# A matrix-vector product of 1024 x 1024 in a one-core backward pass: which operand stands in the array and which streams

## The chip, the cores and the metric

The kernel runs on one core of one Trainium2 chip. The metric is the time of one execution on the device, in microseconds (us); the median of three runs stands for the kernel. The profile comes from one further execution of the same program.

## The reference

The reference is one decode step of an adaLN-conditioned transformer block (one token, width 1024) and its backward pass. Cut to what matters here:

```
mod = silu(c) @ w_mod                      # c: 1x1024, w_mod: 1024 x 6*1024
sa, ca, ga, sb, cb, gb = six rows of 1024 of mod
h = layernorm(x) * (1 + ca) + sa
x = x + ga * attention(h)                  # window of 4096 of a cache of 65536, 32 heads, 4 kv heads
h = layernorm(x) * (1 + cb) + sb
x = x + gb * glu_ffn(h)                    # width 3584
outputs: x and the gradients of x, k_cache, v_cache, wq, wo, w_gate, w_up, w_down, c, w_mod
```

The gradient of c needs, for each of its 1024 rows j, the product of row j of w_mod with the gradient of mod. For the first two sections (sa and ca) that gradient is dh1 and dh1 * ln1, where dh1 is the gradient of the first h and ln1 the first normalised row. So the two products can be folded into one: with w01[j, n] = w_mod[j, n] + w_mod[j, 1024 + n] * ln1[n], the part of the gradient is dcs01[j] = sum over n of w01[j, n] * dh1[n]. This product of a 1024 x 1024 matrix with a row is what the change rewrites.

## The kernel before, in words

Everything is in one program with a hand-written order: each engine runs its instructions in the order of the text, and what crosses engines waits on semaphores. PE multiplies, DVE and ACT move and scale, POOL and SP issue DMAs (POOL on the software queue q0, SP on the hardware queue q1). The outputs are large, above all the two cache gradients (64 MB each), most of which is zeros; the zeros are written all through the run between other transfers. The last pieces of zero are issued on POOL at 459.36 us of the span; after that every transfer is a result that some engine has to make first.

The stretch around the change is the last 90 us of the span. What stands there, in the order of the text:

- `sec(j)` (eight of them): DVE reduces a product with a row (`ttr`, L255), makes an outer product of 128 x 4096 (`outer_dve`, L251), POOL stores it, 1 MB (L1253). `dwq_tile(j)`: an outer product of 128 x 4096 on DVE and a store of 1 MB (L1301). `s2(j)`: an outer product of 128 x 2048 and a store of 0.5 MB (L1305).
- `grad_kv` for the v cache: 32 products of 512 columns on PE (L1288), evacuated by ACT (L1292); then three stores of 1 MB (`kv_store`, L1297).
- `layernorm_bwd_col` (its sums over the partitions by PE, L333, a float32 product), `bcast` (16 products of 128 columns, L346; ACT evacuates, L351).
- **`dcs01 = matvec_T(...)`**, the line of the change. `matvec_T` (L275) has 64 products: block (jb, nb) of the folded matrix `w01_T`, 128 x 128 bf16, is loaded into the array as the weights, and two columns (`dh1_hl[:, nb, :]`, the upper and the lower bf16 half of dh1) stream through. The eight products of one jb add up in PSUM. DVE copies one half (L247) and adds the other (L238).
- `kv_store(out_3, dv_home, 3)` on POOL, then on DVE `sec(7)`, `dwq_tile(3)`, the row x2, two outputs turned by PE (L293), the small sums of the gradient of c (which take `dcs01`), and its output, turned by PE as well.
- `grad_kv` for the k cache: 32 products of 512 columns on PE, evacuated by ACT and DVE in turn; between them DVE makes `dwq_tile(4)` to `dwq_tile(7)` and `s2(0)` to `s2(7)`. `s2(3)` and `s2(4)` write where `sec(7)`'s tile lies, so they wait until its store has landed. The stores go to POOL up to `dwq_tile(5)`, and to SP from `s2(2)` on.
- the last four stores of the k cache, two on POOL and two on SP.

PSUM: the products of 512 columns take their banks from a list of seven that goes round (`new_ps`); small sums take a separate bank (`new_acc`). `scr`, a row of 1024 bf16 per partition, holds `dattn_b` in the last part of the kernel; its last reader there is an outer product of `dwo` on DVE, at 483.5 us.

Of the kernel before, what the change touches and what calls it, by code (L numbers as in the profile page):

```python
# [10 lines left out]
P = 128  # L11
FP32 = mybir.dt.float32
# [8 lines left out]
KD = D // P  # L21
# [40 lines left out]
def kernel(  # L62
# [26 lines left out]
    nc = tc.nc  # L89
# [13 lines left out]
    def ar(off, size):  # L103
        return arena[:, int(off * KIB):int((off + size) * KIB)]
# [4 lines left out]
    def vt(shape, name, dt=FP32):  # L109
        n = shape[1] if dt == FP32 else (shape[1] + 1) // 2  # L110
        if dt not in (FP32, BF16) or n > 48:
            return pool.tile(shape, dt, name=name)
        a = slab[1]
        slab[1] += n
        assert slab[1] <= slab[0].shape[1], slab
        v = slab[0][:, a:a + n]
        return v if dt == FP32 else v.bitcast(BF16)[:, 0:shape[1]]
# [17 lines left out]
    ones_f = vt([P, 1], "ones_f")  # L135
# [83 lines left out]
    def next_pool():  # L219
        nrot[0] += 1  # L220
        return rot[nrot[0] % len(rot)]

    def new_ps(name="ps"):
        p, tag = next_pool()
        return p.tile([P, 512], FP32, name=name, tag=tag)

    def new_bank(name="acc"):
        return pacc.tile([P, 512], FP32, name=name, tag="acc")

    def new_acc(name="acc"):  # L230
        return new_bank(name)[:, 0:64]
# [5 lines left out]
    def tt(out, a, b, op):  # L237
        return nc.vector.tensor_tensor(out=out, in0=a, in1=b, op=op)  # L238
# [4 lines left out]
    def addv(out, a, b):  # L243
        return tt(out, a, b, ALU.add)

    def cp(out, a):
        return nc.vector.tensor_copy(out=out, in_=a)  # L247
# [13 lines left out]
    def hilo(col, n, name):  # L261
        hl = vt([P, n * 2], name, BF16)
        v = hl.rearrange("p (n k) -> p n k", k=2)
        cp(v[:, :, 0], col)
        lo = vt([P, n], name + "_lo")
        tt(lo, col, v[:, :, 0], ALU.subtract)
        cp(v[:, :, 1], lo)
        return v

    def matvec_T(blk, cols, name):  # L270
        ncol = cols.shape[2]
        ps = new_acc("mv_" + name)
        for jb in range(KD):
            for nb in range(KD):
                nc.tensor.matmul(ps[:, jb * ncol:(jb + 1) * ncol], lhsT=blk(jb, nb),  # L275
                                 rhs=cols[:, nb, :], start=(nb == 0), stop=(nb == KD - 1))
        half = ncol // 2
        v = ps[:, 0:KD * ncol].rearrange("p (j n) -> p j n", j=KD)
        res = vt([P, KD * half], name)
        r = res.rearrange("p (j n) -> p j n", j=KD)  # L280
        cp(r, v[:, :, half:ncol])
        addv(r, r, v[:, :, 0:half])
        return r

    def outer_act(out, col, b):
        return nc.scalar.activation(out=out, in_=b, func=ACT.Copy, scale=col)
# [55 lines left out]
    def bcast(col_bf, ncols, out_bf, engs):  # L342
        for k, j0 in enumerate(range(0, ncols, 4)):
            ps = new_ps("bc_ps")
            for jj in range(4):
                nc.tensor.matmul(ps[:, jj * P:(jj + 1) * P],  # L346
                                 lhsT=col_bf[:, j0 + jj:j0 + jj + 1].broadcast_to([P, P]), rhs=ident_bf[:, :],
                                 start=(jj == 0), stop=(jj == 3), skip_group_check=True)
            o = out_bf[:, j0 * P:(j0 + 4) * P]
            if engs[k % len(engs)] == "A":  # L350
                last = nc.scalar.copy(out=o, in_=ps[:, :])  # L351
            else:
                last = cp(o, ps[:, :])
        return last
# [11 lines left out]
    w01_T = ar(128, 16).rearrange("p (n j) -> p n j", n=KD)  # L366
# [193 lines left out]
    for ch in range(8):  # L560
        ps = new_ps("sc_ps")
        for g in range(G):
            mm = nc.tensor.matmul(ps[32 * g:32 * g + 32, 0:512], lhsT=q_col2[:, HG * g:HG * g + 32],
                                  rhs=k_T[:, g, ch * 512:(ch + 1) * 512], start=True, stop=True,
# [157 lines left out]
    for g in range(G):  # L722
        nbank = bank_pair("n_ps", g)
        for t_ in range(KT):
# [7 lines left out]
            for k in range(2):  # L732
                mm = nc.tensor.matmul(nbank[k][:, :], lhsT=k_nat[:, g, t_ * DH:(t_ + 1) * DH],  # L733
                                      rhs=vp[:, t_ % 2, 4 * k:4 * k + 4, :].rearrange("p h d -> p (h d)"),
                                      start=(t_ == 0), stop=False)
# [11 lines left out]
            elif s in (40, 44):  # L747
                j = 6 + (s - 40) // 4
# [3 lines left out]
        for k in range(2):  # L752
            nc.tensor.matmul(nbank[k][:, :], lhsT=nkb_rows[:, :], rhs=bd[:, 4 * k:4 * k + 4, :].rearrange("p h d -> p (h d)"),
                             start=False, stop=True)
# [465 lines left out]
    dattn_b = scr  # L1220
# [75 lines left out]
    def kv_store(og, home, g, queue=nc.gpsimd):  # L1296
        queue.dma_start(out=kv_out(og, g), in_=home[:, g, :])  # L1297
# [11 lines left out]
    for b in range(2):  # L1309
        do4 = new_ps("do4")  # L1310
        for i in range(KD):
            for a in range(4):
                w = wo_t[4 * b + a].rearrange("p a (i d) -> p i a d", i=KD)
                nc.tensor.matmul(do4[32 * a:32 * a + 32, :], lhsT=dattn_bf[:, i:i + 1].broadcast_to([P, 32]),
                                 rhs=w[:, i, :, :], start=(i == 0), stop=(i == KD - 1), tile_position=(0, 32 * a))
        nc.scalar.copy(out=do_sb.rearrange("q (h r a) -> q a h r", h=4, a=4),
                       in_=do4.rearrange("q (a h r) -> q a h r", a=4, h=4))
        for hh in range(4):
            nc.tensor.matmul(dov[:, b, :, hh], lhsT=do_sb[:, hh * P:(hh + 1) * P], rhs=ident_bf[:, 0::32],
                             start=True, stop=True)  # L1320
# [31 lines left out]
    for p in range(NBP):  # L1352
        for it in range(KD):
            nc.tensor.matmul(dh1_ps[:, p:p + 1], lhsT=B_t[p][:, it * P:(it + 1) * P], rhs=dattn_bf[:, it:it + 1],
                             start=(it == 0), stop=(it == KD - 1))
# [16 lines left out]
    zero(Z_ROWS[5])  # L1372
    dw_rows(1, 3, 16, outer_dve)
    dcs234 = matvec_T(lambda jb, nb: w2_t[jb][:, nb * P:(nb + 1) * P], dh2_hl, "dcs234")
    make_bd(DO_bd, do_bf)
    make_bd(Q_bd, q_col2[:, 0:HQ])
    mulv(pd, do_bf, o_col)
    c_ps = new_acc("c_ps")
    for tc_ in range(4):
        nc.tensor.matmul(c_ps[32 * tc_:32 * tc_ + 32, 0:1], lhsT=pd, rhs=ones_f[:, 0:1],  # L1380
                         start=True, stop=True, tile_position=(0, 32 * tc_))
# [18 lines left out]
    dh1_hl = hilo(dh1, KD, "dh1_hl")  # L1400
    for c2 in range(2):
        ps = new_ps("dp_ps")
        for g in range(G):
            for tc_ in range(4):
                t0 = (8 * tc_ + 4 * c2) * P
                nc.tensor.matmul(ps[32 * tc_:32 * tc_ + 32, :], lhsT=do_pad[:, HQ * g:HQ * g + HQ],
                                 rhs=v_nat[:, g, t0:t0 + 512], start=(g == 0), stop=(g == G - 1),
# [21 lines left out]
    dx0 = vt([P, KD], "dx0")  # L1429
    addv(dx0, dx0b, dx1)  # L1430
    bcast(dmod_bf[:, 0:16], 16, dmod_b2, "A")
    dcs01 = matvec_T(lambda jb, nb: w01_T[:, nb, jb * P:(jb + 1) * P], dh1_hl, "dcs01")
    kv_store(out_3, dv_home, 3)
    sec(7)
    dwq_tile(3)
# [5 lines left out]
    dcsum = vt([P, KD], "dcsum")  # L1441
# [6 lines left out]
    ts(t1, t1, 1.0, ALU.add)  # L1448
    mulv(t1, t1, sig_c)
    dct = vt([P, KD], "dct")  # L1450
    addv(dct, dcs01[:, :, 0], dcsum)
    addv(dct, dct, dcs)
    dcv = vt([P, KD], "dcv")
    mulv(dcv, t1, dct)
# [53 lines left out]
```

## Time and profile before

| | us |
|---|---|
| three runs, median (lowest to highest) | 593.28 (592.71 to 594.45) |
| the profiled execution's own time | 593.15 |
| its span (first to last instruction or transfer) | 591.4 |
| the 64 products of L275 on PE, first to last | 535.10 to 536.99 |
| last store issued (POOL) | 571.07 |

The profile gives, for each engine, its busy time, and for each group of instructions what ended the idle time before it. Shares of busy time over the whole span say little here, since stages differ: PE is busy 72% of the span, DVE 60%, ACT 42%, and the DMA engines are at nine tenths or more in all but the first and the last of 40 slices. The views that matter for the change are the timeline from 530 us on, the table of windows of the same stretch (busy time of each engine, granted clock, share and rate of the DMA engines), the source view of single lines (durations, time from the issue of a DMA to its landing) and the DMA view of short windows, which tells which queue's packets moved.

### The profile page before, as it was taken

The numbers are of one execution on the slowest core, as the hardware profiler recorded it, in microseconds if no ns is written. First come the engines' busy times: TensorE is split into PE (matmuls) and PEld (weight loads), VectorE is DVE, ScalarE is ACT, GpSimd is POOL, SyncE is SP. The second block draws the span as 40 slices with busy tenths as digits, with TensorE's granted clock in tenths as the row PEclk, the third lists the DMA queues.
The fourth block names the chain that finished last, engine by engine and source line by source line (L and its number), as shares of the span: only waits on it lengthen the run. The fifth ranks groups of instructions, "written<-read, shape, count | busy, mean of one in ns | idle before, by whom it ended". The sixth has DMA issues, their size and how long they took to land.

```text
span 591.4 us, 10184 instructions
## 1 busy us (share of the span) xinstructions
PE 426.5 (72%) x4167; PEld 245.7 (42%) x4196; DVE 353.6 (60%) x644; ACT 247.9 (42%) x398; POOL 147.3 (25%) x250
## 2 busy tenths in 40 slices
PE   3997779999999999997976856767664447075410
PEld 2784433332334545543544645555552435013100
DVE  3665679988830102039371866877986968555750
ACT  2579511554540103411223655666581456084310
POOL 3112214122122212222222321333212533222100
PEclk9998689999999999998997667786876558555555
DMA  8999999999999999999999999999999999999997
GB/s 348 421 418 423 418 457 423 426 432 434 422 401 462 408 444 427 405 433 442 421 377 414 417 412 410 399 409 402 422 418 423 426 426 423 424 419 415 414 416 313
DMA packets 31903, 246.05 MB, mean 416 GB/s; under 512 B 4765, under 2 KB 4765, under 8 KB 16544
## 3 DMA queue, kind: packets, MB, share of 16 engines
q0 software_dynamic: 26864, 225.98, 94.8%
q1 hardware_dynamic: 4944, 19.41, 9.3%
q8 instruction: 33, 0.54, 0.4%
q14 instruction: 14, 0.11, 0.0%
q10 hardware_dynamic: 48, 0.01, 0.0%
HBM read 88.52 MB, written 185.60 MB: 464 GB/s over the span
## 4 chain that ended last, share of the span: by engine, by line
DMA 36%; PE 27%; DVE 18%; ACT 9%; issue 5%; POOL 1%; ACTq 0%; POOLq 0%; DVEq 0%
DMA out_dram<-out_dram 13%; DMA out_dram<-arena 10%; PE n_ps L733 9%; DMA arena<-in_w_mod_dram 6%; DMA arena<-in_B_w_gate_dram 6%; DVE arena L255 5%; PE b_ps L792 4%; DVE arena L251 4%; PE t_ps L687 4%; DVE scr L255 3%; ACT arena L1292 3%; ACT arena L526 2%; DVE arena L238 2%; ACT arena L695 1%; PE tp_k L505 1%
## 5 line engine op out<-in xcount | busy, mean ns | idle before, releaser
L792 PE MATMUL b_ps<-arena 128*128 128x512 bf16 x493 | 115.3, 382 | 2.6 <-ACT arena L936 1.1
L238 DVE TENSOR_TENSOR arena<-arena 128x2048 bf16<-128x2048 bf16 (+1 forms) x67 | 78.2, 1177 | 9.0 <-PE n_ps L733 5.2
L936 ACT COPY arena<-tp_side 128x1024 bf16<-128x1024 bf16 x62 | 60.8, 1017 | 49.7 <-PE tp_side L935 49.0
L792 PEld LDWEIGHTS <-arena 128*128 128x128 bf16 x512 | 48.7, 99 | 57.6 <-issue 4.6
L733 PE MATMUL n_ps<-arena 128*128 128x512 bf16 x247 | 66.5, 389 | 3.4 <-DVE arena L238 2.5
L202 POOL DMA_DIRECT2D out_dram<-out_dram x72 | 35.7, 496 | 129.5 <-PE n_ps L733 49.6
L251 DVE TENSOR_SCALAR arena<-arena,slab 128x3584 bf16<-128x3584 bf16 (+2 forms) x40 | 43.4, 1120 | 24.1 <-DMA out_dram<-arena 24.1
L935 PE MATMUL tp_side<-ident_bf,arena 128*128 128x128 bf16 x496 | 49.7, 265 | 8.9 <-DVE arena L238 4.5
L935 PEld LDWEIGHTS <-arena 128*128 128x128 bf16 x496 | 41.3, 122 | 17.7 <-issue 9.2
L1288 PE MATMUL ps_kv<-arena 32*128 32x512 bf16 x64 | 26.6, 581 | 28.5 <-DVE arena L259 11.7
L695 ACT CAST arena<-t_ps 128x512 bf16<-128x512 f32 x56 | 28.9, 598 | 39.9 <-PE t_ps L687 39.9
L1292 ACT ACTIVATE arena<-ps_kv 128x512 bf16<-128x512 f32 x48 | 25.0, 723 | 38.8 <-PE ps_kv L1288 19.7
L255 DVE CUSTOM_DVE_ANT_0 arena<-arena,scr 128x1024 bf16<-128x1024 bf16 x35 | 40.8, 1219 | 0.2
L733 PEld LDWEIGHTS <-arena 128*128 128x128 bf16 x256 | 21.5, 99 | 35.4 <-issue 18.9
L255 DVE CUSTOM_DVE_ANT_0 scr<-arena,b1k 128x1024 bf16<-128x1024 bf16 x28 | 34.2, 1222 | 3.1 <-DMA arena<-in_B_w_down_dram 2.6
L247 DVE CAST arena<-b_ps 128x512 bf16<-128x512 f32 x6 | 4.1, 692 | 48.9 <-PE b_ps L792 48.9
L209 POOL DMA_DIRECT2D out_dram<-out_dram x32 | 19.5, 610 | 33.6 <-DVE rows_all L238 25.2
L687 PE MATMUL t_ps<-arena 128*32 128x512 bf16 x256 | 24.1, 399 | 3.3 <-ACT arena L756 2.8
L1288 PEld LDWEIGHTS <-arena 32*128 32x128 bf16 x64 | 6.8, 112 | 47.1 <-issue 46.4
L526 ACT COPY arena<-tp_wq 128x1024 bf16<-128x1024 bf16 x23 | 21.4, 1070 | 7.3 <-PE tp_wq L524 7.3
L1073 ACT COPY arena<-tp_ug 128x1024 bf16<-128x1024 bf16 x21 | 20.5, 1007 | 7.5 <-PE tp_ug L1072 7.5
L1049 PE MATMUL fg<-arena,slab 128*32 128x256 bf16 x224 | 15.1, 404 | 8.2 <-DMA arena<-in_B_w_gate_dram 8.2
(266 smaller groups left out, 649.3 us busy)
## 6 DMA issues: line engine op xcount, KB each, us to landing
out_dram<-arena POOLq DMA_DIRECT2D x35, 1024.0 KB, 14.6
out_dram<-out_dram POOLq DMA_DIRECT2D x32, 1024.0 KB, 12.8
out_dram<-arena POOLq DMA_DIRECT2D x16, 896.0 KB, 17.5
out_dram<-zeros POOLq DMA_DIRECT2D x10, 1024.0 KB, 10.3
arena<-in_A_wq_dram POOLq DMA_DIRECT2D x8, 1024.0 KB, 20.9
arena<-in_A_wo_dram POOLq DMA_DIRECT2D x8, 1024.0 KB, 13.7
arena<-in_w_mod_dram POOLq DMA_DIRECT2D x7, 1024.0 KB, 18.9
arena<-in_B_w_up_dram POOLq DMA_DIRECT2D x14, 512.0 KB, 10.1
```

Source lines behind the costliest of these rows:

```text
L202: ins = nc.gpsimd.dma_start(out=as_rows(region, BIGP).bitcast(FP32), in_=zero_src[:, 0:P * ZW // 4].rearrange("i (p x) -> (i p) x", p=BIGP ...
L238: return nc.vector.tensor_tensor(out=out, in0=a, in1=b, op=op)
L251: return nc.vector.tensor_scalar(out=out, in0=a, scalar1=s1, scalar2=None, op0=op0)
L255: return nc.vector.tensor_tensor_reduce(out=out, in0=w, in1=b, scale=1.0, scalar=0.0, op0=ALU.mult, op1=ALU.add, accum_out=acc)
L687: nc.tensor.matmul(ps[32 * hh:32 * hh + 32, :].rearrange("p (j m) -> p j m", j=4), lhsT=N_sb[:, h * P + a:(h + 1) * P - 3 + a:4], rhs=a4[: ...
L695: nc.scalar.copy(out=o, in_=v)
L733: mm = nc.tensor.matmul(nbank[k][:, :], lhsT=k_nat[:, g, t_ * DH:(t_ + 1) * DH], rhs=vp[:, t_ % 2, 4 * k:4 * k + 4, :].rearrange("p h d -> ...
L792: mm = nc.tensor.matmul(bbank[p][k][:, :], lhsT=a4[:, p, h, :], rhs=wo_t[u][:, a, k * 512:(k + 1) * 512], start=(i == 0 and a == 0), stop= ...
L935: nc.tensor.transpose(tp[:, i * P:(i + 1) * P], blk[:, i * P:(i + 1) * P], ident_bf[:, :])
L936: nc.scalar.copy(out=blk if dst is None else dst, in_=tp[:, :])
L1288: nc.tensor.matmul(ps[:, :], lhsT=rows[r, t8 * P:(t8 + 1) * P], rhs=bd[r, :], start=True, stop=True, tile_position=(32 * tc_, 0))
L1292: nc.scalar.activation(out=o, in_=v, func=ACT.Copy, scale=float(scale))
```

## The change

`dcs01` is made by a new function, in which the two columns of dh1 stand in the array as weights and the folded matrix streams through, 512 columns at a time. Per half h of the 1024 rows j: eight products of 512 columns add up in the first two partitions of a bank; DVE copies the two rows of 512 to SBUF, as float32, into `scr`; four float32 products with a column of two ones turn 128 columns each into a column of 128 partitions and add the two rows. One copy then takes the eight columns out. The addition of the two halves on DVE goes away, since the ones add them. Nothing else is moved; the line numbers behind the new function are 16 higher.

```
+    def matvec_rows(mat, cols, name, room):
+        row = room.bitcast(FP32)[0:2, 0:512]
+        col = new_acc("mc_" + name)
+        for h in range(2):
+            ps = new_ps("mr_" + name)
+            for nb in range(KD):
+                nc.tensor.matmul(ps[0:2, :], lhsT=cols[:, nb, :], rhs=mat(nb)[:, h * 512:(h + 1) * 512],
+                                 start=(nb == 0), stop=(nb == KD - 1))
+            cp(row, ps[0:2, :])
+            for j in range(4):
+                nc.tensor.matmul(col[:, 4 * h + j:4 * h + j + 1], lhsT=row[:, j * P:(j + 1) * P],
+                                 rhs=ones_f[0:2, 0:1], start=True, stop=True)
+        res = vt([P, KD], name)
+        cp(res, col[:, 0:KD])
+        return res
...
-    dcs01 = matvec_T(lambda jb, nb: w01_T[:, nb, jb * P:(jb + 1) * P], dh1_hl, "dcs01")
+    dcs01 = matvec_rows(lambda nb: w01_T[:, nb, :], dh1_hl, "dcs01", dattn_b)
...
-    addv(dct, dcs01[:, :, 0], dcsum)
+    addv(dct, dcs01, dcsum)
```

## The prediction

> **What bounds the kernel now.** I read the busy shares by slice first, then the timeline from 530 us, the table of windows for the same stretch, and the times from issue to landing of the stores. The slices:
>
> ```profile
> PE   3997779999999999997976856767664447075410
> PEclk9998689999999999998997667786876558555555
> DMA  8999999999999999999999999999999999999997
> ```
>
> A digit is tenths of a slice of 14.8 us. The DMA engines are full in all slices but the ends: 246 MB at 416 GB/s fill the span. A delay on another engine costs something only if the transfers run out of work, and it is the last slices that have no zeros left to fill in (the last piece is issued at 459.36). The change lies in slice 37:
>
> ```profile
> 534.99 1.91 PEld L275 LDWEIGHTS <-arena 128*128 128x128 bf16 x64
> 535.10 1.89 PE L275 MATMUL mv_dcs<-arena 128*128 128x2 bf16 x64
> ...
> 537.03 0.17 DVE L247 COPY arena<-mv_dcs 128x8 f32<-128x8 f32 x1 [2.46 <-PE mv_dcs L275]
> ...
> 537.31 1.22 DVE L255 CUSTOM_DVE_ANT_0 g_last<-g_last,arena 128x1024 bf16<-128x1024 bf16 x1
> ...
> 540.03 1.02 POOL L1253 DMA_DIRECT2D out_dram<-arena  x1 [1.77 <-DVE arena L251]
> ...
> 548.60 0.53 POOL L1301 DMA_DIRECT2D out_dram<-arena  x1 [6.84 <-DVE arena L251]
> ...
> 557.63 0.75 DVE L251 TENSOR_SCALAR arena<-arena,slab 128x2048 bf16<-128x2048 bf16 x1 [4.35 <-DMA out_dram<-arena]
> ```
>
> Start and duration in us; in brackets, the idle time before and what ended it. DVE waits for the 64 products and has `sec(7)` behind them (537.31), whose store POOL issues at 540.03. `dwq_tile(3)` follows at 541.23, and then POOL has nothing until `dwq_tile(4)`, 548.60. The 557.63 row is `s2(3)`, which waits for `sec(7)`'s landing. The windows (PE, PEld, DVE, ACT, POOL busy, then granted clock, DMA share, GB/s):
>
> ```profile
> 520.00:530.00 10.00, 9.28 (x19) 1.88 (x19) 5.90 (x6) 9.92 (x21) 2.34 (x3) 0.50 1.02 421
> 535.00:540.00 5.00, 1.99 (x67) 1.90 (x65) 2.94 (x6) 2.81 (x6) 2.10 (x4) 0.50 1.02 415
> 555.00:560.00 5.00, 0.37 (x1) 0.10 (x1) 2.37 (x4) 0.00 (x0) 0.00 (x0) 0.50 1.00 413
> 588.00:591.40 3.40, 0.00 (x0) 0.00 (x0) 0.00 (x0) 0.00 (x0) 0.00 (x0) 0.50 0.11 48
> ```
>
> The clock is 0.50 throughout, and at 535 to 540 the transfers go on at full rate with every engine idle two fifths of the time or more: they live on what was issued earlier.
>
> **What goes.** 64 products in 1.89 us (0.0265 us each at this clock) and one small addition on DVE.
>
> **What comes, on PE and DVE in turn.** A product of 512 columns starts every 0.427 us at this clock (the k-cache products of L1288, from 544.90 on), and the last ends 0.629 us after its start (their duration). Eight take 7 x 0.427 + 0.629 = 3.62. They start at 535.10 as before: their bank was last held by the third from last of the 32 v-cache products, which ACT has evacuated by 534.9. DVE's copy of 512 float32 columns takes 0.69 (the 128x512 f32 copies of L247; 8x128 takes 0.28, so columns set it, not partitions). DVE starts 0.04 behind PE; PE starts 0.12 (L293) to 0.28 (L643) behind DVE, I take 0.2. `scr` was last read at 483.5, so the copy waits for nothing else. Four float32 products are eight passes, as L829 shows two each: 0.11 per pass there at full clock, 0.07 and 0.17 between L333's at half clock, 0.22 if L829's doubles. I take 0.17, L333's own, and keep 0.07 and 0.22. So:
>
> - half one: 535.10 + 3.62 = 538.72; copy to 539.45; turn from 539.65, 8 x 0.17 to 541.0.
> - half two: to 544.62; copy to 545.35; turn from 545.55, seven passes and 0.42 for the last (L333) to 547.2; the copy of eight columns, and `sec(7)` starts at 547.3.
>
> Before it starts at 537.31, so DVE is **10.0 us late** (8.5 with the short passes, 11.0 with the long ones and 0.28). Behind DVE's wait stand `sec(7)`, `dwq_tile(3)`, x2, the sums, the k cache's evacuation and all later outer products; PE's turns and k-cache products stand behind theirs. All of it shifts by 10.0, `dwq_tile(4)`'s issue to 558.6.
>
> **What hides it.** First, `s2(3)`'s wait: its input would be ready at 553.28 + 10.0 = 563.3, `sec(7)` has landed at about 557.6 (below), so from there the chain is only 563.3 - 557.63 = 5.7 late: last stores at 575.7 to 576.8 instead of 570.07 to 571.07. Second, the backlog. Stores on POOL's queue go in order; `sec(7)`, issued at 550.0, still meets the v cache's stores, the last of which lands at 537.73 + 17.34 = 555.06 (L1297's longest). It lands at 557.6 as before, and `dwq_tile(3)` 2.55 later (the spacing of the landings before it), at 560.15; before it takes longer,
>
> ```profile
> L1301 POOL DMA_DIRECT2D out_dram<-arena x1: 532/532/532, 541.2 to 541.2; - x1
> ...
> DMA to landing us min/median/max: 19.7/19.7/19.7
> ```
>
> 541.23 + 19.7 = 560.9, since SP's first store shares the engines from 557.9 on, which it won't now. Then **nothing is queued** until `dwq_tile(4)`.
>
> A store counts as landed when the slowest of its 16 engines is done, and the spread is large: by the trace's landing counts the 16 parts of `dwq_tile(3)` landed between 554.8 and 560.9, half of them by 557.9, and those of the very last store between 584.4 and 590.45. The end is set by the slowest engines (the 588 to 591.4 window: share 0.11). So the faster engines can idle from 555 or 558 to about 560 and still end no later than the slow ones do; only a gap on the slow ones lengthens the run.
>
> Their gap is 558.6 + L - 560.15, L being the time from issue to a first packet on an idle queue. Before shows L from two sides: SP's first load, with idle engines, is issued at 0.74 and has no packet by 1.70 (first at 1.74), so 1.0; the last k-cache stores on POOL are issued at 570.55 and move nothing before 575, while SP's packets fill the engines, so 4.45. The engines that matter are nearly empty, so it is near the first; I take 2.0, for the software queue's issue is longer (0.53 on POOL, 0.33 on SP). Gap: 558.6 + 2.0 - 560.15 = **0.4 us**. Ends: 557.1 + 1.0, no gap; 559.6 + 4.45, 3.9 us.
>
> Later gaps: from 560.6 the stores of `dwq_tile(4)` to `s2(3)` are 4 MB, 10.1 us; the next, `dwq_tile(6)`, is issued at 562.0 + 5.7 = 567.7. No gap there, nor before the last four.
>
> The Trainium skill ("DMA: Bandwidth & Descriptors", Specifications) gives a first-byte latency of about 1 us for a software queue. By it the gap is nil and the time 593.15; the 4.45 us row speaks against it, though for busy engines.
>
> **Sum.** 593.15 (profiled execution) + 0.4 = 593.55; it is 0.13 below the median of the runs, so 593.7.
>
> **Rivals.**
> 1. *The queue runs dry on the slow engines too.* A gap longer than 1.8 us (0.3%, about what a measurement of this kernel can tell from no change) needs delay and L to sum to 13.4 instead of 12.0, as with 10.0 and the 4.45 of the POOL row: 558.6 + 4.45 - 560.15 = 2.9, 596.2; with both at their ends 597.2. For it: that is the only POOL row with an empty queue, and if slow engines are merely behind in turn, the mean one counts (558.6 + 2.0 - 558 = 2.6, 595.9). Against: other queues filled the engines in that row.
> 2. *A shorter delay.* If PE gets its full clock, product starts halve to 0.21: the two halves take about 3.4 us less, the delay is 6.6, `dwq_tile(4)` is issued at 555.2, before the queue empties: 593.3. Against: the clock stays at 0.50 though PE is 9.28 of 10 us busy at 520 to 530. The Trainium skill ("TensorE: Matmul & The Clock Gate", Part 1: The HAM clock gate) says about 3.4 us of sustained matmuls release the clock; by that the 520 window should show it, and it doesn't.
> 3. *Faster.* From 585 on only SP's queue has work, and the rate falls (365 GB/s, then 221, 115, 49): 1.12 MB in 5.4 us that 415 GB/s would move in 2.7. When the faster engines idle at 555 to 560 and the last stores join a shorter SP queue, the end can be more even. Half of the 2.7 gained: 592.0. Against: each engine's bytes are the same.
> 4. *That the change isn't what it says*: excluded by the built order on PE, 16 products of 2x512 and eight of 128x1 in place of 64.
>
> **Chances.** Forecast (gap under 1.8 us) 0.48, rival 2 0.06, both within 0.3%; rival 1 0.38; rival 3 0.08. So faster 0.08, same 0.54, slower 0.38. The range leaves out a tenth at each end: from rival 3's 592.2 to rival 1's 596.8.
>
> **What would show it.** Right: the copy out of the turn at about 547.1 and `sec(7)` at 547.3; PE waiting on DVE twice; `s2(3)` at 563 with no wait on a DMA; a DMA share well below 1 in 555 to 561 alone; last stores issued near 576, the span's end within a microsecond. Wrong: product starts nearer than 0.427 or a granted clock over 0.50 (delay), DMA idle past 561 or in other windows (L, supply), or an end that moves by more than the gap on the engines that end last.

## The result, and the profile after

The median of 22 runs of the changed kernel is **594.06 us** (592.99 to 595.37), that of 22 runs of the kernel before, taken in turn with them, 593.35 us (592.19 to 594.60). The ratio is 1.0015, with a 95% interval of 1.0008 to 1.0021: a little slower, by less than the 0.3% of the forecast's bound. The profiled execution took 594.23 us (before 593.15), and its span is 592.42 us (before 591.37), so 1.05 us more; the medians differ by 0.71 us.

The slices of the page of the changed kernel, in the same rows as before:

```profile
PE   3997689998999999997977756776665447086520
PEclk9997689999999999999998757778777657557555
DMA  8999999999999999999999999999999999999996
```

The fourth digit from the end is the slice of the change. PEclk is 7 there, and was 5. The DMA row differs in the last digit alone.

The timeline of the changed kernel from the first new product on (start, duration, what; in brackets the idle time before and what ended it):

```profile
535.16 3.27 PE L291 MATMUL mr_dcs<-arena 128*2 128x512 bf16 x8
...
538.47 0.68 DVE L247 COPY scr<-mr_dcs 2x512 f32<-2x512 f32 x1 [3.98 <-PE mr_dcs L291]
...
539.21 1.05 PE L295 MATMUL mc_dcs<-slab,scr 2*128 2x1 f32 x8 [0.77 <-DVE scr L247]
...
540.19 1.89 PE L291 MATMUL mr_dcs<-arena 128*2 128x512 bf16 x8
542.11 0.68 DVE L247 COPY scr<-mr_dcs 2x512 f32<-2x512 f32 x1 [2.96 <-PE mr_dcs L291]
...
544.01 1.22 DVE L255 CUSTOM_DVE_ANT_0 g_last<-g_last,arena 128x1024 bf16<-128x1024 bf16 x1
...
546.73 1.02 POOL L1269 DMA_DIRECT2D out_dram<-arena  x1 [8.55 <-DVE arena L251]
...
555.29 0.53 POOL L1317 DMA_DIRECT2D out_dram<-arena  x1 [6.83 <-DVE arena L251]
...
558.03 2.60 DVE L251 TENSOR_SCALAR arena<-arena,slab 128x4096 bf16<-128x4096 bf16 x3
...
572.80 1.05 POOL L1313 DMA_DIRECT2D out_dram<-arena  x2 [12.66 <-issue]
```

The first eight products take 3.27 us and the second eight 1.89, since the granted clock rose at 538.0, near the end of the first eight. `sec(7)` starts at 544.01 instead of 537.31, which makes DVE 6.70 us late, and `dwq_tile(4)` is issued at 555.29 instead of 548.60. At 558.03 the outer products run on with no wait for a DMA: the 4.35 us that `s2(3)` waited before have gone. So the last two stores on POOL start only 2.25 us later than before (572.80 for 570.55).

The windows of the changed kernel (busy PE, PEld, DVE, ACT, POOL, then granted clock, DMA share, GB/s):

```profile
535.00:540.00 5.00, 4.23 (x18) 1.63 (x16) 0.68 (x1) 2.73 (x6) 2.10 (x4) 0.70 1.01 410
540.00:545.00 5.00, 3.12 (x19) 1.72 (x18) 1.75 (x3) 0.00 (x0) 0.00 (x0) 0.98 1.00 418
...
535.10:538.00 2.90, 2.90 (x9) 0.84 (x8) 0.00 (x0) 2.63 (x6) 1.92 (x4) 0.50 0.99 415
538.00:542.00 4.00, 3.23 (x18) 1.55 (x16) 0.68 (x1) 0.00 (x0) 0.18 (x1) 1.00 1.01 408
...
554.00:556.00 2.00, 0.86 (x5) 0.14 (x1) 2.00 (x3) 1.74 (x4) 0.58 (x2) 0.50 0.86 358
556.00:558.00 2.00, 1.02 (x3) 0.48 (x4) 2.00 (x4) 0.41 (x1) 1.02 (x2) 0.50 0.93 381
...
588.00:592.40 4.40, 0.00 (x0) 0.00 (x0) 0.00 (x0) 0.00 (x0) 0.00 (x0) 0.50 0.05 20
```

The kernel before has, at 554 to 558:

```profile
554.00:556.00 2.00, 0.00 (x0) 0.00 (x0) 0.00 (x0) 0.00 (x0) 0.00 (x0) 0.50 1.03 422
556.00:558.00 2.00, 0.00 (x0) 0.00 (x0) 0.37 (x1) 0.00 (x0) 0.00 (x0) 0.50 0.97 406
```

The granted clock is 0.70 and 0.98 at 535 to 545, where it was 0.50. The DMA engines fall to 0.86 and 0.93 at 554 to 558 (before 1.03 and 0.97), a mean idle time of 2 x 0.14 + 2 x 0.07 = 0.42 us. It falls on the fast engines only: `dwq_tile(3)` has landed, on its slowest engine, at 559.64 and `dwq_tile(4)` at 562.16, which is 2.52 us later, the usual spacing of full queues. And in this execution the transfers end **earlier** than in that of the kernel before: SP's last store has landed at 590.06 (before 590.45), with 16 parts that end between 586.79 and 590.06 instead of 584.38 and 590.45.

So the time isn't lost in the transfers. It is lost behind them. The last landing of POOL's queue is the issue of its last store and the time to its landing, 573.33 + 15.07 = 588.40 after and 571.07 + 14.23 = 585.30 before. It moved by 3.10 us, 0.84 more than the issue. The wait for a first packet is not what added this: the first packet of these two stores moved 4.90 us after the first one's issue before (575.45) and 4.96 after (577.76), with SP's packets on the engines until then. The rest passed between that packet and the landing, 9.86 us before and 10.64 after, while SP's queue moved about as many bytes as POOL's; why it took longer is not shown. What follows on POOL is the program's last line. The source view of it in the kernel before, on POOL (shortest, median and longest of three in ns, then when the first and the last start):

```profile
L1503 POOLq DRAIN  x3: 51/93/17575, 571.0 to 591.1; - x3
```

The same view of the changed kernel:

```profile
L1519 POOLq DRAIN  x3: 51/93/18418, 573.2 to 592.1; - x3
```

The longest is the first: POOL waits for its own DMA queue. Before, that ends at 571.0 + 17.6 = 588.5, after at 573.2 + 18.4 = 591.6, both **3.24 us after POOL's last store has landed**. 0.78 us of a last round between the engines follow. On SP, the DRAINs of the kernel before and of the changed one:

```profile
L1503 SPq DRAIN  x3: 7/7/7, 590.5 to 590.8; - x3
...
L1519 SPq DRAIN  x3: 7/7/7, 590.1 to 591.9; - x3
```

Before, SP's last landing (590.45) came later than 588.5 and 0.92 us after it the span was over; now SP is through at 590.2 and waits, and it is POOL's closing that comes last: 588.40 + 3.24 + 0.78 = 592.42, the span. It grew by 1.05 us though every byte was out 0.4 us sooner.

### The profile page after: what moved, and what is told of

Same layout as the page of the kernel before. It is cut to its first block, busy times and chain, and to the rows that moved or that the text cites. A ratio compares the mean times of both kernels' runs of the same rounds, so it can differ in the third digit from the quotient of the medians.

```text
span 592.4 us, 10121 instructions
## 1 busy us (share of the span) xinstructions
PE 432.1 (73%) x4135; PEld 246.2 (42%) x4164; DVE 354.6 (60%) x645; ACT 247.9 (42%) x398; POOL 147.0 (25%) x250
## 4 chain that ended last, share of the span: by engine, by line
PE 44%; DVE 20%; DMA 19%; ACT 7%; issue 6%; POOL 1%; ACTq 0%; POOLq 0%; DVEq 0%
PE b_ps L808 15%; DMA out_dram<-arena 9%; PE n_ps L749 8%; DMA arena<-in_B_w_gate_dram 5%; DVE arena L251 5%; DVE arena L238 4%; PE t_ps L703 3%; DMA arena<-in_w_mod_dram 3%; DVE arena L255 3%; PE ps_kv L1304 3%; DVE scr L255 2%; ACT arena L542 2%; PE bc_ps L362 1%; ACT arena L711 1%; PE tp_k L521 1%
## 5 line engine op out<-in xcount | busy, mean ns | idle before, releaser
L977 POOL DMA_DIRECT2D arena<-in_B_w_up_dram x14 | 10.8, 770 | 42.9 <-DVE slab L255 22.1
## 6 DMA issues: line engine op xcount, KB each, us to landing
arena<-in_w_mod_dram POOLq DMA_DIRECT2D x7, 1024.0 KB, 18.7
```

## The experiments

**Theory A**: POOL's closing step sets the end as soon as POOL's last landing is less than 3.1 us ahead of SP's (4.02 us from landing to end against 0.92); before it was 5.14 ahead, after 1.66. The change only makes POOL's last stores late enough for it. **Theory B**, the rival: the loss is not one of the end. It is what the new products and the transfers around them cost in themselves, with a gap in the supply of the DMA engines where the delay is long enough, and no choice of a queue for the last stores alters it. For the clock, **R**: it rose because the new products fill all 128 rows of the array, where the cache products fill 32; **S**: the rows do not matter, and any products issued as closely as these would raise it.

### The last four stores on another queue, in the changed kernel

```
-        kv_store(out_2, dk_home, g, nc.gpsimd if g < 2 else tail)
+        kv_store(out_2, dk_home, g, tail)
```

> The changed kernel, with the last four stores of the k cache all on SP's queue instead of two on POOL and two on SP. Theory A (closing): in the changed kernel the transfers end as early as before (590.06 against 590.45 us), and the span is longer because POOL's closing step takes 3.24 us after the last store of its own queue has landed, and that landing has moved from 585.30 to 588.40. Then without a late store on POOL the span should end about 0.9 us after SP's last landing, near 591.0, 1.4 us less than the changed kernel: 592.8, ratio to the kernel before 0.998 to 1.000. Theory B (gap, the forecast's own step): the slow DMA engines were short of work at 555 to 560; moving the last stores gives nothing back: 594.1, ratio 1.0015.

Measured 593.36 us (592.82 to 593.74), ratio 1.0002 (0.9993 to 1.0011): level with before, though this interval alone still meets that of the change at its edge. The source view of the last line in this kernel, on POOL:

```profile
L1519 POOLq DRAIN  x3: 51/93/12812, 559.1 to 591.5; - x3
```

The same on SP:

```profile
L1519 SPq DRAIN  x3: 7/7/7, 590.9 to 591.2; - x3
```

POOL's step is over at 559.1 + 12.8 = 571.9 and out of the way. SP's first DRAIN is at 590.9, though its last store landed at 590.03: SP goes through the semaphores of the DMAs in nine steps, one after the other, and its last store's is now in the third, so the six steps behind it come after the landing; before, it was in the last. From the landing to the DRAIN it is 0.87 us instead of 0.09, and 0.45 of it lies between the third step and the fourth, which is not explained here. That is 0.8 us which the change of queue costs in itself, as this run of the kernel before with the same edit shows:

> The kernel before with the last four stores of the k cache all on SP, the control to the same edit of the changed kernel. Theory A (closing): POOL's closing step ends 2 us ahead of SP's last landing there, so that there is nothing to win: 593.2, ratio 1.000. If one queue at the end is better in itself, the ratio is below 0.999, and what the same edit won in the changed kernel was not the closing step.

Measured 594.07 us (592.99 to 594.79), ratio 1.0017 (1.0007 to 1.0027). I had expected no difference: the edit costs the kernel before 0.17%. Its span is 592.68, 1.70 after its last landing at 590.98, where before has 0.92; the rest of the 1.31 us by which the span is longer is a last landing 0.53 us later. So what the edit gives back in the changed kernel is more than the 0.13% seen. To be rid of the 0.8 us, I tried the hardware queue of ACT for the two stores of POOL, in the changed kernel and in the one before:

```
-        kv_store(out_2, dk_home, g, nc.gpsimd if g < 2 else tail)
+        kv_store(out_2, dk_home, g, nc.scalar if g < 2 else tail)
```

> The changed kernel with the two last k-cache stores that POOL issues put on ACT's hardware queue, SP's two left as they are. Theory A (closing): POOL's closing step is done by about 572, and SP's last store is still the last one SP looks at, so the 0.8 us that four stores on SP cost at the end don't come; the span should end about 0.9 us after the last landing near 590.1, at 591.0: 592.7, ratio 0.999. If ACT's queue has a closing step of its own like POOL's, it stays near 1.0015. If late transfers on any queue cost it, likewise.

> The kernel before with the two last k-cache stores that POOL issues put on ACT's hardware queue: the control. Theory A (closing): POOL's closing step was not what ended it (2 us ahead), so nothing to win: 593.0, ratio 1.000, and the changed kernel with the same edit is no slower than this one. If the edit is better in itself, the ratio is under 0.999 here too.

Measured 593.29 us, ratio 0.9999 (0.9990 to 1.0007), and 593.11 us, ratio 1.0003 (0.9993 to 1.0013). The source view of the last line on POOL, in the first and in the second:

```profile
L1519 POOLq DRAIN  x3: 51/93/12122, 559.6 to 591.4; - x3
...
L1503 POOLq DRAIN  x3: 51/102/24205, 552.6 to 591.6; - x3
```

POOL's step is over at 571.7 and 576.8. SP still needed 0.9 us from its last landing to its DRAIN in both (its last store's semaphore was in the third step again), so the 592.7 was not reached. But the pair settles the main point: with POOL's closing out of the way in both, the changed kernel is level with the other one, and its interval doesn't meet that of the change itself (1.0008 to 1.0021). B is out for a delay of this size.

### The closing step alone, in the kernel before

```
-        kv_store(out_2, dk_home, g, nc.gpsimd if g < 2 else tail)
+        kv_store(out_2, dk_home, g, nc.gpsimd)
```

> The kernel before, with the last four stores of the k cache all on POOL's queue. Nothing on PE, DVE or ACT is changed, and no byte more is moved. Theory A (closing): POOL's last landing becomes the last of all, near 590, its closing step ends 3.24 us later, the span near 594: 2.5 us more, 595.9, ratio 1.004. Theory B (gap): the last stores' queue doesn't matter, 593.4, ratio 1.000.

Measured 596.65 us (596.42 to 597.28), ratio 1.0057 (1.0043 to 1.0070). The source view of the last line, on POOL:

```profile
L1503 POOLq DRAIN  x3: 51/102/22138, 571.7 to 594.3; - x3
```

The last byte is out at 590.50, as before (590.45), and POOL's step ends at 571.7 + 22.1 = 593.8, 3.32 us later. No work is changed here, only the queue that lands last, and it costs 0.57%, against 0.4% expected.

### The delay alone, in the kernel before

Fourteen additional outer products of 1024 columns on DVE, where the new products would be, into a row that nothing reads any more; 30 of them in a second kernel.

```
     dcs01 = matvec_T(...)
+    for _ in range(14):
+        outer_dve(scr, ones_f[:, 0:1], dq_b[:, 0:1024])
```

> The kernel before with its 64 products, and 14 additional outer products of 128x1024 on DVE (0.478 us each by the rows of L251) behind the two copies of dcs01: a delay of 6.7 us alone, of the same size as in the changed kernel. They write an unused row. Theory A (closing): the delay alone brings the whole difference: dwq_tile(4)'s store is issued at 555.3, the last stores at 572.3, POOL's last landing is near 588.4 and the time as that of the changed kernel, 594.1, ratio 1.0015. Theory B (gap): 555.3 + 2.0 lies ahead of 560.15, where the slow engines run out, so no gap: 593.4, ratio 1.000. If it is something about the products themselves (their form, or the clock they bring) and not the delay, the ratio is 1.000 too, with POOL's last landing at 585.

Measured 594.74 us (594.23 to 595.13), ratio 1.0024 (1.0016 to 1.0033). The timeline of this kernel:

```profile
537.21 7.26 DVE L251 TENSOR_SCALAR scr<-arena,slab 128x1024 bf16<-128x1024 bf16 x14
544.39 1.22 DVE L255 CUSTOM_DVE_ANT_0 g_last<-g_last,arena 128x1024 bf16<-128x1024 bf16 x1
```

The source view of the last line, on POOL:

```profile
L1505 POOLq DRAIN  x3: 51/93/18742, 573.6 to 592.8; - x3
```

A delay of 7.08 us with the 64 old products gives the loss of the change and 0.09% more, with intervals that meet: POOL's step ends at 573.6 + 18.7 = 592.3, again 3.24 after POOL's last landing (589.10). That is 0.7 us later than in the changed kernel, 0.4 by the later issue and 0.3 by a longer time to landing. The clock stayed at 0.50 in this stretch. So no new product is needed for the loss; lateness of this size is enough.

> The kernel before with 30 additional outer products on DVE behind the copies of dcs01: a delay of 15.2 us (14 of them made 7.1, 0.506 each), past the point from which the slow DMA engines too should run out of work. They write an unused row. With 1.1 us from issue to first packet on an idle queue (seen in the run with 32 rows): sec(7)'s store is issued at 555.2, its first packet comes at 556.3, while the slowest engine is free at about 554.8; dwq_tile(4)'s at 563.8, first packet 564.9, while dwq_tile(3) ends at about 561.4. Theory A (closing) alone: about 3 us, as POOL's last store ends with SP's: 596.4, ratio 1.005. Theory B (gap) alone: 1.5 + 3.5 = 5.0 us, 598.3, ratio 1.0085. Both, one after the other: 8 us, 601.4, ratio 1.0135.

Measured 602.80 us (602.71 to 603.33), ratio 1.0169 (1.0155 to 1.0182), 1.4 us above what I had expected from both theories together. With a delay of 15.9 us (0.4 of it because this execution entered the stretch later) the queues do run dry, twice; windows of this kernel:

```profile
552.00:554.00 2.00, 0.00 (x0) 0.00 (x0) 1.93 (x4) 0.00 (x0) 0.00 (x0) 0.50 0.35 147
554.00:556.00 2.00, 0.00 (x0) 0.00 (x0) 2.00 (x4) 0.00 (x0) 0.06 (x1) 0.50 0.00 0
556.00:558.00 2.00, 0.59 (x2) 0.12 (x2) 1.41 (x5) 0.00 (x0) 1.49 (x2) 0.50 0.31 131
...
562.00:564.00 2.00, 2.00 (x9) 0.83 (x8) 1.84 (x3) 1.49 (x3) 0.00 (x0) 0.50 0.34 133
564.00:566.00 2.00, 0.07 (x1) 0.00 (x0) 2.00 (x4) 1.21 (x3) 1.24 (x3) 0.50 0.30 111
```

What the shares lack of 1 in these five windows of 2 us is 7.4 us, and the last byte is out at 597.53, 7.1 later than before: here the idle time comes out at the end nearly in full. With the closing step in place of SP's end (3.24 + 0.78 - 0.92 = 3.1) that makes the 10.2 us by which the span is longer (601.55). My expectation had both dry spells, at 1.5 and 3.5 us. The second came so: `dwq_tile(4)` landed 5.96 us after `dwq_tile(3)` (569.13 for 563.17) instead of 2.5. The first was too short: no packet moved from 553.8 to 557.5, since the slowest engine was free at 554.1 and not at 554.8, and `sec(7)`'s store, issued at 555.94, had its first packet 1.6 us later and not 1.1.

### The clock: the same products over 32 rows

```
-  nc.tensor.matmul(ps[0:2, :], lhsT=cols[:, nb, :], rhs=mat(nb)[:, h * 512:(h + 1) * 512], ...)
+  nc.tensor.matmul(ps[0:2, :], lhsT=cols[0:32, nb, :], rhs=mat(nb)[0:32, h * 512:(h + 1) * 512], ...,
+                   tile_position=(0, 0))
```

Three quarters of each sum are left out here.

> The changed kernel, its 16 products of 512 columns taking 32 of the 128 rows only, so that three quarters of the sum are left out; the columns that stream, and so the time of a product at a given clock, are the same. Theory R (rows): the clock rose to full at 538 because products on all 128 rows filled the array long enough; the 32-row products of the v cache had not brought it at 520 to 533. Then the clock stays at 0.50, a product starts every 0.427 us, sec(7) starts at 547.3 and dwq_tile(4)'s store is issued at 558.6, as the forecast had it; by theory A (closing) the last stores are then issued at 575.7, POOL's last landing comes near 590 and the span near 594, 1.5 us over the changed kernel: 595.6, ratio 1.004; by theory B (gap) alone it is the forecast's 0.4 us, 593.8, ratio 1.0007. Theory S (any stream): products back to back bring the clock whatever their rows; then all is as in the changed kernel: sec(7) at 544.0, 594.1, ratio 1.0015.

Measured 597.87 us (597.42 to 598.30), ratio 1.0073 (1.0060 to 1.0086). The timeline of this kernel:

```profile
541.89 3.57 PE L291 MATMUL mr_dcs<-arena 32*2 32x512 bf16 x8
...
548.21 1.21 DVE L255 CUSTOM_DVE_ANT_0 g_last<-g_last,arena 128x1024 bf16<-128x1024 bf16 x1
```

Its windows (columns as above):

```profile
540.00:545.00 5.00, 4.89 (x16) 2.58 (x16) 0.05 (x1) 0.00 (x0) 0.00 (x0) 0.50 1.00 416
...
558.00:560.00 2.00, 1.06 (x6) 0.30 (x3) 2.00 (x4) 1.74 (x4) 0.51 (x1) 0.50 0.12 47
560.00:562.00 2.00, 0.83 (x3) 0.36 (x4) 2.00 (x4) 0.41 (x2) 1.09 (x3) 0.50 0.79 328
```

R holds: the clock stays at 0.50 from 506 us to the end, with PE 4.89 of 5 us busy, every product starts 0.427 us after the one before, the turn takes 0.22 us a pass, and `sec(7)` starts at 548.21. The other kernel with 32 rows (below) shows the same; in the four kernels of this document with 128 rows the clock rose, at 537.17 to 538.59. One thing stays untested: the edit also names a tile of the array (`tile_position`), as the cache products do, so the rows filled and a mode of the array that goes with it are not told apart. This execution entered the stretch 0.54 us late, so the delay is 548.21 - 537.31 - 0.54 = 10.4 us. This is the kernel that the forecast had in mind, and its gap can be read: `dwq_tile(4)` is issued at 559.49, no packet moves from 559.5 to 560.6, and it lands 3.94 us after `dwq_tile(3)` (563.73 for 559.79) instead of 2.52, so 1.4 us are lost on the slowest engine. The last byte is out at 592.50, and POOL's step follows, in the source view of the last line:

```profile
L1519 POOLq DRAIN  x3: 51/93/18317, 577.4 to 596.2; - x3
```

577.4 + 18.3 = 595.7, and 0.78 make the span of 596.5: 591.37 + 0.54 + 1.5 at the last byte + 3.1 for the closing. R with A was the nearest of the expectations, and 2.3 us short. The same kernel with the last four stores on SP, as in the first experiment:

> The kernel with 32-row products (three quarters of the sum left out; delay 10.4 us, a gap of 1.4 us seen on the slowest DMA engine) with the last four stores all on SP. Theories A and B each take their part: without a late store on POOL the 3.1 us of the closing step go and the gap of about 1.5 us stays: 594.7, ratio 1.0025. If the closing step were not what ends it, it stays at 1.0073; if there were no gap, it would come down to 1.000.

Measured 594.55 us (594.14 to 594.83), ratio 1.0029 (1.0018 to 1.0041), 0.15 off. POOL's step is over at 563.0 + 9.6 = 572.6, by the same view of this kernel:

```profile
L1519 POOLq DRAIN  x3: 51/102/9634, 563.0 to 592.4; - x3
```

### The new products behind `sec(7)` and `dwq_tile(3)`

Neither needs `dcs01`; only the small sums behind them do.

```
-    dcs01 = matvec_rows(lambda nb: w01_T[:, nb, :], dh1_hl, "dcs01", dattn_b)
     kv_store(out_3, dv_home, 3)
     sec(7)
     dwq_tile(3)
+    dcs01 = matvec_rows(lambda nb: w01_T[:, nb, :], dh1_hl, "dcs01", dattn_b)
```

> The changed kernel with the 16 products and eight turns as they are, but DVE's copies of them placed behind sec(7) and dwq_tile(3), so that neither waits for PE. Theory A (closing, by the delay): sec(7) starts at 534.6, its store is issued at 537.3; x2 and what follows is some 3 us late (copies end at 543.9 instead of x2's start at 540.9), which s2(3)'s wait of 4.35 us takes up, so the last stores are issued near 570.1 as before, POOL's last landing is near 585.3 and the time that of the kernel before: 593.2, ratio 1.000. If the products cost something in themselves (the clock, PE's work), it stays at the changed kernel's 1.0015.

Measured 592.99 us (592.19 to 593.61), ratio 1.0002 (0.9993 to 1.0010). The timeline of this kernel:

```profile
534.95 1.22 DVE L255 CUSTOM_DVE_ANT_0 g_last<-g_last,arena 128x1024 bf16<-128x1024 bf16 x1
535.69 2.96 PE L291 MATMUL mr_dcs<-arena 128*2 128x512 bf16 x8
...
551.97 0.53 POOL L1317 DMA_DIRECT2D out_dram<-arena  x1 [11.18 <-DVE arena L251]
```

The source view of its last line, on POOL:

```profile
L1519 POOLq DRAIN  x3: 51/93/18322, 570.7 to 591.0; - x3
```

`sec(7)` runs beside the products, `dwq_tile(4)` is 3.4 us later than before instead of 6.7, and the last stores are issued at 569.79 to 570.79, no later than before. POOL's step ends at 570.7 + 18.3 = 589.0, ahead of SP's last landing at 590.38, and the loss is gone with all 16 new products still there. No version that I tried beats the kernel before: this one and the two with the last stores elsewhere are level with it.

## Why the prediction was right, and where it was not

- **What bounds the kernel**: right. The transfers do, and a delay costs only what it does to them or behind them.
- **The delay, 10.0 us**: wrong, 6.70 measured. The step that failed is the one that kept the clock at 0.50 because PE was 9.28 of 10 us busy at 520 to 530. That window was no witness: its products fill 32 rows (and start every 0.49 us, where the new ones start every 0.427). With 32 rows the new products keep 0.50 too and the delay is 10.4; with 128 rows the clock was 1.0 from 538.0 on, and rival 2's 6.6 us and 555.2 came out as 6.70 and 555.29. The delay depends on when the clock rises: every change of the granted clock in these traces lies a multiple of 3.41 us from every other in its trace, wherever the products start. With the entry taken out it was 6.8 us here, 6.4 in the kernel with the last stores on SP (rise at 537.17) and 7.1 in that with ACT (538.59). Of the other terms, the copies were right (0.68 for 0.69), PE behind DVE was too long (0.06 for 0.2), and a pass of the turn at half clock is 0.22, the upper bound and not the 0.17 taken. The Trainium skill ("TensorE: Matmul & The Clock Gate", Part 1: The HAM clock gate) gives about 3.4 us of sustained matmuls for the release of the clock; the 4.6 us from the first of the 16 full-height products of `bcast` (533.37), which the new ones follow, to 538.0 agree with it. The 12 us of 32-row products that left the clock at 0.50 do not: that section of the Trainium skill does not speak of rows, and here they decide (or the array tile that went with them in the 32-row kernels).
- **What hides it**: right. `s2(3)`'s wait went, and took 6.70 down to 2.25 at the last stores.
- **The gap of 0.4 us on the slow engines**: not there, as the delay was shorter. Its parts held: `dwq_tile(3)` landed at 559.64 (560.15 forecast), the fast engines idled first and at no cost, and with the longer delay of the 32-row kernel the slow ones lost 1.4. There L was 1.1 us, next to the lower of the two rows given and not 2.0; 559.49 + 1.1 - 559.79 would be 0.8, so the sum still came out short. The Trainium skill's first-byte latency of about 1 us for a software queue ("DMA: Bandwidth & Descriptors", Specifications) agrees with the 1.1; the kernel with 30 outer products has 1.1 once and 1.6 once. The upper row of L was misread: POOL's queue was not empty at 570.55, since `dwq_tile(5)` on it landed at 574.00, and the first packet of the later stores moved at 575.45, so it is 4.9 and not 4.45.
- **The sum**: no term for what an engine does behind its last store. The end was taken as the last landing plus a constant, and that constant belongs to the queue. POOL's is 4.02 us (3.24 + 0.78), SP's 0.92. This is the step that decided the sign, and all of the 1.05 us. That 593.7 stands near 594.06 is owed to a forecast gap that did not come and a closing step that was not forecast. It is luck as far as the mechanism goes: the rise of the clock had been given a chance of 0.06, and the kernel in which the clock stays at 0.50, which is the one that the forecast worked out, takes 597.87, above the upper end of the range (596.8).
- **Rivals**: 2 was right on the delay and, for want of the closing step, 0.8 too low on the time. 3's more even end came, as 0.4 us at the last byte, and was hidden by POOL's step. 1 is real at longer delays (the 30 outer products) and did not apply.

## What to carry to other kernels

Where transfers bound a kernel to its end, look not only for the last byte but for the queue that carries it and what its engine still does: here POOL's last landing must be 3.1 us ahead of SP's, or its closing step is what ends the program. Before calling a clock fixed, compare the rows that the products fill, not only how busy PE is. And when an edit makes an engine's wait longer, put ready work that doesn't need the result ahead of the wait.

## What the runs showed of the hardware

- The step in which POOL closes its software DMA queue ended 3.16 to 3.32 us after the queue's last landing in all twelve kernels: 3.16 where none of the last four stores were on it (five kernels), 3.24 where two were (six), 3.32 where four were (one). SP's DRAIN came 0.09 us after its last landing in the kernel before, and 0.87 to 0.89 where the last store's semaphore stood in the third of the nine steps that SP goes through (five kernels).
- 16 matmuls with two columns as weights raised the clock if they filled 128 rows and did not if they filled 32, at the same spacing at the start (0.427 us).
- An idle software queue on idle DMA engines had its first packet 1.1 us after the issue where the issue took 0.53 us, and 1.6 where it took 1.02; on engines that another queue fills it took 5.0 us (572.80 to 577.76).
- The 16 parts of one store ended up to 6 us apart (584.38 to 590.45), and a mean DMA share of 0.86 at 554 to 556 cost nothing at the last byte.

Open are why some DMA engines are behind the others, why POOL's last stores took 0.8 us longer from their first packet to the landing, what exactly the clock gate counts, and what POOL does in its 3.24 us.
